# Expert stage of an attention, mixture-of-experts and MLP kernel: one matrix's loads issued one per unit, and the next expert's first token blocks transposed in units 0, 2, 3 and 5

## The chip, the cores and the metric

The kernel runs on one core of a Trainium2 chip. The metric is the device time of one execution in microseconds. The engines are named as in the profile: PE (TensorE matrix multiplies), PEld (its weight loads), DVE (VectorE), ACT (ScalarE), POOL (GpSimd) and SP (SyncE, which here only issues DMA transfers). Each engine runs its instructions in the order in which the program hands them over.

## The reference

Three stages run one after the other on 4608 rows of 512 numbers. Only the second one is touched.

```python
def _moe_ref(x, w_gate, w_noise, noise, w1, w2):   # x: (4608, 512), 8 experts, w1: (8, 512, 1024), w2: (8, 1024, 512)
    ...                                            # noisy logits; the two best experts of a row and their weights
    for e in range(E):
        for k in range(2):
            mask = top2[:, k] == e
            h = np.maximum(x[mask] @ w1[e], 0.0)
            out[mask] += top2_w[mask, k, None] * (h @ w2[e])
```

Before it stands an attention with pooled keys and values, and the gate. After it stands a dense layer, `(h - tanh(h)) @ w_out` with `h = x @ w_in`. All three come back in 32 bits; the two matrix products of an expert run as three 16-bit products each, on values split into a high and a low half.

## The kernel before, in words

**Units.** Function `moe` walks over 8 experts. An expert has room for 1216 rows, in three groups of 512, 384 and 320 rows. A group takes 8 units, so expert e has units 0 to 23; its third group (320 rows) has units 16 to 23. The names `f` (0 to 7, the unit within the group) and the keys `(e, unit)` count them. One unit is written out as: `L1` (12 matmuls into the PSUM tile `ph`, lines 355 to 357; then `ACT L359` and `DVE L360` make the two halves of `hT`), `tr` if a block is due in this unit, `L2` of two units earlier (`LAG = 2`, lines 377 to 384), and then the jobs hung on this unit with `at`. `ph` has two buffers, so `L1` of a unit waits until `DVE L360` of the unit two before has read its buffer.

**Transposing.** `tr(i, j)` prepares block j of group i while the group before it runs. ACT and DVE write the halves of 128 rows into the tile `xp` (lines 341 and 342), SP issues a transposing DMA from `xp` into `xTp` (line 343), and POOL gathers the block after next into `xg` (line 315). `xp` has one buffer: the next `ACT L341` cannot write it before the DMA has read it. A group of 512 rows has four blocks, one of 384 or 320 rows has three. Blocks are due in the units where `j * KF // n == f`: for four blocks these are f = 0, 2, 4 and 6, for three blocks 0, 2 and 5. The only groups with four blocks are the first ones of each expert; their blocks come up while the third group of the expert before runs.

**The next expert's matrices.** `Prep` loads a matrix in four chunks of 512 KB into the tile `stage` (line 118 for the first matrix, line 120 for the second), takes the largest absolute value of each chunk (`amax`, DVE line 127, and after the fourth the line 130 that makes `cm`), turns this into a scale (`fin1` with the PE transpose of `cm` on line 170, `fin2`), and splits the chunks into `pair` (ACT line 154, DVE line 159). For the first matrix the load is in unit 0, `amax` in units 3 to 6; for the second one the load is in unit 13, `amax` of chunks 0 and 1 in unit 18 and of 2 and 3 in unit 19, `fin1` in unit 20. Expert 0 has the first matrix's jobs four units later.

**Other jobs that the text names.** `Y` writes a finished group through the tile `ys` (three buffers) to `y_d` (SP line 409). For experts 1 to 4, `Conv.split` in units 1 and 2 also writes through `ys` (ACT line 290, DVE line 291) to `ws_d` (SP line 293). Line 225 loads pieces of the third stage's matrix.

Of the kernel before, what the change touches and what calls it, by code (L numbers as in the profile page):

```python
# [37 lines left out]
def kernel(ctx, tc, q, k, v, w_gate, w_noise, noise, w1, w2, w_in, w_out, out):  # L38
# [54 lines left out]
    with ExitStack() as st:  # L93
        moe(nc, tc, st, V, z)
# [81 lines left out]
def both(g):  # L176
    for _ in g:
        pass
# [8 lines left out]
def moe(nc, tc, st, V, z):  # L187
# [8 lines left out]
    KD, KF = DM // 128, FF // 128  # L196
# [7 lines left out]
    for e in range(E):  # L204
        c = 0
# [91 lines left out]
    def at(key, f, *a):  # L297
        jobs.setdefault(key, []).append((f, a))

    def run_jobs(key, between):  # L300
        for f, a in jobs.pop(key, []):
            f(*a)
            between()
# [3 lines left out]
    def gather(k):  # L307
        if k < len(blocks):
            e, c, n = blocks[k]
            if k == 6:  # L310
                x = wk.tile([128, 2, DM], F16, name="xp", bufs=1).rearrange("p a n -> p (a n)").bitcast(F32)
            else:
                x = wk.tile([128, DM], F32, name="xg", bufs=2)
            XG[k] = x
            nc.gpsimd.indirect_dma_start(  # L315
                out=x[:n], out_offset=None, in_=x_d[:, :],
                in_offset=bass.IndirectOffsetOnAxis(ap=idx[:n, e, c:c + 1], axis=0))
# [7 lines left out]
    def tr(i, j):  # L325
        if j == 0:
            XTP[i] = wk.tile([128, 2, KD, 512], F16, name="xTp")
        x = XG.pop(first[i] + j)
        n = blocks[first[i] + j][2]
        if i == 1:  # L330
            p = ps.tile([128, KD, 128], F32, name="pt", bufs=2)
            for m in range(KD):
                nc.tensor.transpose(p[:, m, :n], x[:n, 128 * m:128 * m + 128], identf[:n, :n])
            o = XTP[i][:, :, :, 128 * j:128 * j + n]
            nc.scalar.activation(o[:, 0], p[:, :, :n], AF.Copy)
            tt(o[:, 1], p[:, :, :n], o[:, 0], op=OP.subtract)  # L336
            if j < 2:
                gather(7 + j)
            return
        xp = wk.tile([128, 2, DM], F16, name="xp", bufs=1)  # L340
        nc.scalar.activation(xp[:n, 0], x[:n], AF.Copy)  # L341
        tt(xp[:n, 1], x[:n], xp[:n, 0], op=OP.subtract)  # L342
        nc.sync.dma_start_transpose(XTP[i].rearrange("p a m n -> p (a m) n")[:, :, 128 * j:128 * j + n],
                                    xp[:n].rearrange("p a n -> p (a n)"))
        gather(first[i] + j + 2)
# [3 lines left out]
    def L1(i, f):  # L349
        e, g, c0, nt = groups[i]  # L350
        w, x = W[e, 1].pair, XTP[i]
        p = ps.tile([128, 512], F32, name="ph", bufs=2)
        for m in range(KD):
            s = slice(128 * f, 128 * f + 128)
            nc.tensor.matmul(p[:, :nt], w[:, 0, m, s], x[:, 0, m, :nt], start=(m == 0), stop=False)  # L355
            nc.tensor.matmul(p[:, :nt], w[:, 0, m, s], x[:, 1, m, :nt], start=False, stop=False)  # L356
            nc.tensor.matmul(p[:, :nt], w[:, 1, m, s], x[:, 0, m, :nt], start=False, stop=(m == KD - 1))  # L357
        h = HC[i, f] = wk.tile([128, 2, 512], F16, name="hT", bufs=5)
        nc.scalar.activation(h[:, 0, :nt], p[:, :nt], AF.Relu)  # L359
        stt(h[:, 1, :nt], p[:, :nt], 0.0, h[:, 0, :nt], op0=OP.max, op1=OP.subtract)  # L360
# [3 lines left out]
    def L2(i, f):  # L364
        e, g, c0, n = groups[i]
        w, h = W[e, 2].pair.rearrange("p a b (c n) -> p a (b c) n", n=DM), HC[i, f]
        nb, half = divmod(n, 128)
        if f == 0:
            if g == 0:
                SC[e] = wk.tile([128, 1], F32, name="ysc")  # L370
                tt(SC[e], W[e, 1].sc[:, 1:2], W[e, 2].sc[:, 0:1], op=OP.mult)
            for j in range(nb + (half > 0)):
                PY[i, j] = ps.tile([128, DM], F32, name="py", bufs=4)
        for j in range(nb):
            s = slice(128 * j, 128 * j + 128)
            p = PY[i, j]
            nc.tensor.matmul(p, h[:, 0, s], w[:, 0, f], start=(f == 0), stop=False)  # L377
            nc.tensor.matmul(p, h[:, 0, s], w[:, 1, f], start=False, stop=False)  # L378
            nc.tensor.matmul(p, h[:, 1, s], w[:, 0, f], start=False, stop=(f == KF - 1))  # L379
        if half and f % 2:  # L380
            terms = [(u, a, b) for u in (f - 1, f) for a, b in ((0, 0), (0, 1), (1, 0))]
            for k, (u, a, b) in enumerate(terms):
                q = 64 * (k % 2)
                nc.tensor.matmul(PY[i, nb][q:q + 64], HC[i, u][:, a, 128 * nb:n], w[:, b, u],
                                 start=(f == 1 and k < 2), stop=(f == KF - 1 and k > 3))
        if not half:
            del HC[i, f]
        elif f % 2:
            del HC[i, f - 1], HC[i, f]
        if f == KF - 1 and i > 0:  # L390
            Y(i)
# [161 lines left out]
    for e in range(E):  # L553
        if e + 1 < E:
            c1, c2 = PR[e + 1, 1], PR[e + 1, 2]
            d = 4 if e == 0 else 0
            at((e, d), c1.load)
            at((e, 7 + d), lambda c=c1: both(c.fin1()))
            at((e, 8 + d), lambda c=c1: both(c.fin2()))
            for c in range(4):  # L560
                at((e, 3 + d + c), c1.amax, c)
                at((e, (12 if d else 10) + c), c1.split, c)
                at((e, 18 + c // 2), c2.amax, c)
                at((e, 22 + c // 2), c2.split, c)
            at((e, 15 if d else 13), c2.load)
            at((e, 20), lambda c=c2: both(c.fin1()))
            at((e, 21), lambda c=c2: both(c.fin2()))
        cv = Conv(e // 4, e % 4)
        for j in range(8):
            u = j + 3 if 0 < e < 5 else (j + 2 if j < 6 else j + 4) if e + 1 < E else (j + 4 if j < 5 else j + 6)  # L570
            if j < 2:
                at((e, j + 2 * (e + 1 == E)), cv.load, j)
            at((e, u), cv.conv, j)
            if j + 2 < 8:
                at((e, u), cv.load, j + 2)
        at((e, 14), cv.stat)
        at((e, 15), cv.fin1)
        at((e, 16), cv.fin2)
        at((e, 16), cv.norm)
        for j in range(4):  # L580
            at((e, 20 + j // 2), cv.split, j)
            if cv.which == 0:
                if j == 0:
                    at((e + 1, 0), cv.combos)
                at((e + 1, 1 + j // 2), cv.split, j, True)
# [11 lines left out]
    for u in range(len(units) + LAG):  # L597
        if u < len(units):
            i, f = units[u]
            L1(i, f)  # L600
            if u < KF:
                gate(4)
            n = -(-groups[i + 1][3] // 128) if i + 1 < len(groups) else 0
            if i > 0:
                for j in range(n):
                    if j * KF // n == f:
                        tr(i + 1, j)
            elif f == KF - 1:
                while not V["idx_loaded"]:
                    gate(10 ** 6, True)  # L610
                for k in range(4, 7):
                    gather(k)
        if u >= LAG and u not in (KF, KF + 1):
            L2(*units[u - LAG])
        if u == KF - 1:
            L2(*units[u - 1])
            L2(*units[u])
            for j in range(n):
                tr(1, j)
        if u in (KF, KF + 1):  # L620
            Y(0, range(2 * (u - KF), 2 * (u - KF) + 2))
        if u > LAG and units[u - LAG - 1][1] == KF - 1 and groups[units[u - LAG - 1][0]][0:2] == (E - 2, len(SIZES) - 1):
            overflow()
        if u in (1, 3):
            V["first"][1].split((u + 3) // 2)
        if u < KF:
            gate(6, u > 1)
        if u == KF + LAG:
            V["early"].close()
            V["pairs"].append(V["ew"].enter_context(tc.tile_pool(name="ew1", bufs=1, side="right")))  # L630
        if u < len(units):
            run_jobs((groups[i][0], KF * groups[i][1] + f), lambda: u < KF and gate(4))
            if u < KF:
                gate(6)
# [1086 lines left out]
```

## Time and profile before

| | before |
|---|---|
| median of 3 runs | 1829.58 us (1828.01 to 1830.68) |
| the profiled execution: time | 1828.06 us |
| its span, first to last instruction | 1826.2 us |
| PE busy | 1763.6 us (97% of the span) |
| DVE busy | 1301.2 us (71%) |
| ACT busy | 940.9 us (52%) |
| mean granted clock of TensorE | 0.992 |

The span is what the trace covers; the device time is 1.86 us longer. In the rows below, times are microseconds from the span's start. A number in square brackets is how long the engine had stood idle before the instruction, with what ended the wait behind the arrow. `SPq` is an issue on SP's queue: its second number is how long the issue took, not the transfer.

### The profile page before, as it was taken

What the parts mean: (1) busy time and instruction counts of PE and PEld (TensorE: products, weight loads), DVE (VectorE), ACT (ScalarE), POOL (GpSimd) and SP (SyncE); (2) the same over time, 40 slices, a digit from 0 to 9 for tenths busy, and PEclk for the clock granted to TensorE, in tenths of its full rate; (3) what the DMA queues carried; (4) which work ended last, traced back from release to release, by engine and by line L of the source; (5) the groups of instructions that cost most, each with busy time, mean ns of one, the idle gap of its engine ahead of it and who ended that gap; (6) DMA issues with size and microseconds to landing.
All of it is one profiled execution on the core that took longest, in us unless ns stands there. A gap on an engine that the chain in (4) does not pass through costs nothing. (4 is left out here: it accounts for less than half of the span.)

```text
span 1826.2 us, 28991 instructions
## 1 busy us (share of the span) xinstructions
PE 1763.6 (97%) x10791; PEld 1077.7 (59%) x10792; DVE 1301.2 (71%) x2640; ACT 940.9 (52%) x2249; POOL 263.2 (14%) x258
## 2 busy tenths in 40 slices
PE   7998889999999999999999999999999999999998
PEld 5998874445445454545445454566666666666664
DVE  5788867776676667566566456687878879787775
ACT  5886732443434343443424245565766657666554
POOL 2222001312113030110101012110111201010000
PEclk8999989999999999999999999999999999999999
DMA  9867223464464545454544434531313313041100
GB/s 224 236 166 205 61 74 108 141 161 130 141 187 122 183 129 165 139 147 124 146 106 121 103 110 120 118 89 34 93 38 74 83 42 91 24 93 46 37 24 25
DMA packets 264158, 203.45 MB, mean 111 GB/s; under 512 B 188160, under 2 KB 208640, under 8 KB 264000
## 3 DMA queue, kind: packets, MB, share of 16 engines
q1 hardware_dynamic: 251840, 162.16, 33.0%
q0 software_dynamic: 11904, 38.81, 8.2%
q8 instruction: 88, 1.44, 0.3%
q14 instruction: 70, 0.57, 0.1%
q10 hardware_dynamic: 256, 0.46, 0.1%
HBM read 121.82 MB, written 45.74 MB: 92 GB/s over the span
## 5 line engine op out<-in xcount | busy, mean ns | idle before, releaser
L359 ACT ACTIVATE hT<-ph 128x512 f16<-128x512 f32 (+2 forms) x192 | 96.8, 505 | 425.0 <-PE ph L357 418.8
L355 PE MATMUL ph<-xTp,pair 128*128 128x384 f16 (+2 forms) x736 | 245.2, 333 | 14.0 <-DMA xTp<-xp 4.8
L356 PE MATMUL ph<-xTp,pair 128*128 128x384 f16 (+2 forms) x736 | 244.9, 333 | 0.4 <-DVE xTp L336 0.4
L357 PE MATMUL ph<-xTp,pair 128*128 128x384 f16 (+2 forms) x736 | 244.9, 333 | 0.0
L360 DVE SCALAR_TENSOR_TENSOR hT<-ph,hT 128x512 f16<-128x512 f32 (+2 forms) x192 | 110.8, 577 | 163.3 <-ACT hT L359 161.5
L1042 PE MATMUL py<-wo,gT 128*128 128x512 f16 x576 | 218.3, 379 | 1.0 <-issue 1.0
L1040 PE MATMUL py<-wo,gT 128*128 128x512 f16 x576 | 218.3, 379 | 0.1
L377 PE MATMUL py<-pair,hT 128*128 128x512 f16 x576 | 218.3, 379 | 0.0
L378 PE MATMUL py<-pair,hT 128*128 128x512 f16 x576 | 218.3, 379 | 0.0
L379 PE MATMUL py<-pair,hT 128*128 128x512 f16 x576 | 218.3, 379 | 0.0
L1041 PE MATMUL py<-wo,gT 128*128 128x512 f16 x576 | 218.3, 379 | 0.0
L899 PEld LDWEIGHTS <-wi 128*128 128x128 f16 x1536 | 150.3, 98 | 58.5 <-issue 0.2
L315 POOL DMA_INDIRECT xg<-x_d,idx x75 | 85.5, 1139 | 669.8 <-DVE xp L342 462.3
L713 POOL DMA_INDIRECT y<-y_d,ridx x64 | 78.9, 1233 | 518.5 <-DVE y L724 240.7
L355 PEld LDWEIGHTS <-pair 128*128 128x128 f16 x768 | 75.0, 98 | 83.6 <-issue 24.9
L356 PEld LDWEIGHTS <-pair 128*128 128x128 f16 x768 | 75.1, 98 | 61.8 <-issue 6.0
L357 PEld LDWEIGHTS <-pair 128*128 128x128 f16 x768 | 75.1, 98 | 57.1 <-issue 0.6
L999 ACT ACTIVATE th<-th,bias 128x512 f32<-128x512 f32 x144 | 102.5, 712 | 3.3 <-DVE th L997 1.6
L1000 DVE SCALAR_TENSOR_TENSOR th<-th,t 128x512 f32<-128x512 f32 x144 | 98.6, 684 | 1.4 <-ACT th L999 1.4
L989 DVE TENSOR_TENSOR gT<-th,gT 128x512 f16<-128x512 f32 x144 | 98.7, 685 | 0.2 <-ACT gT L988 0.2
L996 DVE SCALAR_TENSOR_TENSOR t<-hb,cinf,hs 128x512 f32<-128x512 f32 x64 | 48.0, 749 | 70.9 <-ACT hs L995 68.8
L1314 ACT ACTIVATE at<-psc,mx 128x72 f32<-128x72 f32 x288 | 87.8, 334 | 18.6 <-DVE mx L1303 18.6
(305 smaller groups left out, 3496.6 us busy)
## 6 DMA issues: line engine op xcount, KB each, us to landing
stage<-in_moe_w SPq DMA_DIRECT2D x64, 512.0 KB
y_d<-ys SPq DMA_DIRECT2D x82, 256.0 KB
x_d<-xr SPq DMA_DIRECT2D x36, 256.0 KB
out<-o SPq DMA_DIRECT2D x36, 256.0 KB
qt<-in_q SPq DMA_DIRECT2D x32, 256.0 KB
raw<-in_moe_w_in SPq DMA_DIRECT2D x32, 256.0 KB
raw<-in_moe_w_out SPq DMA_DIRECT2D x32, 256.0 KB
kt<-in_k SPq DMA_DIRECT2D x7, 768.0 KB
```

The source lines that it names most:

```text
L355: nc.tensor.matmul(p[:, :nt], w[:, 0, m, s], x[:, 0, m, :nt], start=(m == 0), stop=False)
L356: nc.tensor.matmul(p[:, :nt], w[:, 0, m, s], x[:, 1, m, :nt], start=False, stop=False)
L357: nc.tensor.matmul(p[:, :nt], w[:, 1, m, s], x[:, 0, m, :nt], start=False, stop=(m == KD - 1))
L360: stt(h[:, 1, :nt], p[:, :nt], 0.0, h[:, 0, :nt], op0=OP.max, op1=OP.subtract)
L377: nc.tensor.matmul(p, h[:, 0, s], w[:, 0, f], start=(f == 0), stop=False)
L378: nc.tensor.matmul(p, h[:, 0, s], w[:, 1, f], start=False, stop=False)
L379: nc.tensor.matmul(p, h[:, 1, s], w[:, 0, f], start=False, stop=(f == KF - 1))
L899: nc.tensor.matmul(p, w[:, a, m], y[:, c, b, m], start=(start and m + x == 0), stop=(m == 1 and x == 2), skip_group_check=True)
L999: nc.scalar.activation(q, q, AF.Square, bias=bias[:, 2:3], scale=SP5)
L1040: nc.tensor.matmul(p, g[:, 0, s], wo[:, 0, f], start=(f == 0), stop=False)
L1041: nc.tensor.matmul(p, g[:, 0, s], wo[:, 1, f], start=False, stop=False)
L1042: nc.tensor.matmul(p, g[:, 1, s], wo[:, 0, f], start=False, stop=(f == KF - 1))
```

## The change

The loads of the first matrix of the next expert go out one chunk per unit, in units 0 to 3 (4 to 7 for expert 0), in place of four at once. And a group of four blocks has them transposed in units 0, 2, 3 and 5 in place of 0, 2, 4 and 6.

```diff
@@ -554,7 +554,8 @@
             d = 4 if e == 0 else 0
-            at((e, d), c1.load)
+            for c in range(4):
+                at((e, d + c), c1.load, [c])
             at((e, 7 + d), lambda c=c1: both(c.fin1()))
@@ -603,7 +604,7 @@
                 for j in range(n):
-                    if j * KF // n == f:
+                    if ((0, 2, 3, 5)[j] if n == 4 else j * KF // n) == f:
                         tr(i + 1, j)
```

On DVE, in units 18 to 21 of an expert, the second block's two instructions move up. The rows begin with the two `amax` of unit 18; `L360` is one row for each unit.

```order
 L127 TENSOR_REDUCE am<-stage 128x1 x2
 L360 SCALAR_TENSOR_TENSOR hT<-ph,hT 128x320
+L342 TENSOR_TENSOR xp<-xg,xp 128x512
 L127 TENSOR_REDUCE am<-stage 128x1 x2
 L130 TENSOR_REDUCE cm<-am 128x1
 L360 SCALAR_TENSOR_TENSOR hT<-ph,hT 128x320
-L342 TENSOR_TENSOR xp<-xg,xp 128x512
 L173 TENSOR_REDUCE cx<-pt 1x1
 L291 SCALAR_TENSOR_TENSOR wi<-qf,wsc,wi 128x512 x2
 L360 SCALAR_TENSOR_TENSOR hT<-ph,hT 128x320
+L342 TENSOR_TENSOR xp<-xg,xp 128x512
```

Block 2 (`L342`) now stands ahead of the last two `amax` and of `L130`; block 3 moves from unit 22 to the end of unit 21. On ACT, from the same unit 18 on, the order is:

```order
 L359 ACTIVATE hT<-ph 128x320
 L341 ACTIVATE xp<-xg 128x512
-L359 ACTIVATE hT<-ph 128x320 x2
-L341 ACTIVATE xp<-xg 128x512
+L359 ACTIVATE hT<-ph 128x320
+L341 ACTIVATE xp<-xg 128x512
+L359 ACTIVATE hT<-ph 128x320
 L290 ACTIVATE wi<-qf,wsc 128x512 x2
 L359 ACTIVATE hT<-ph 128x320
+L341 ACTIVATE xp<-xg 128x512
```

Between the `L341` of block 1 and that of block 2 there is now one `L359` where there were two. On SP, in units 0 to 2 of expert 1, the order before was:

```order
L118 DMA stage<-in_moe_w 128x1024 x4
L225 DMA raw<-in_moe_w_in 128x512
L409 DMA y_d<-ys 128x512 x2
L409 DMA y_d<-ys 64x512
L293 DMA ws_d<-ys 256x1x512 x2
L225 DMA raw<-in_moe_w_in 128x512
L343 DMA_TRANSPOSE xTp<-xp 128x8x128
```

At the same place it now is:

```order
L118 DMA stage<-in_moe_w 128x1024
L225 DMA raw<-in_moe_w_in 128x512
L409 DMA y_d<-ys 128x512 x2
L409 DMA y_d<-ys 64x512
L293 DMA ws_d<-ys 256x1x512 x2
L118 DMA stage<-in_moe_w 128x1024
L225 DMA raw<-in_moe_w_in 128x512
L343 DMA_TRANSPOSE xTp<-xp 128x8x128
L293 DMA ws_d<-ys 256x1x512 x2
L118 DMA stage<-in_moe_w 128x1024 x2
```

One load stands ahead of the `y_d` writes instead of four. PE and POOL run the same instructions in the same order as before.

## Rows read from the trace of the kernel before

**Rows 1.** Busy time by engine in the stretch 375 to 1000 us, clock, DMA.
```profile
375.00:1000.00 625.00, 612.51 (x3245) 307.20 (x3245) 406.80 (x802) 244.99 (x450) 93.92 (x81) 1.00 0.52 145
```
**Rows 2.** Waits of PE in that stretch: us in total, times, longest.
```profile
PE ph L355 <- DMA xTp<-xp: 4.8, 4, 1.4
PE ph L355 <- DVE pair L159: 3.8, 3, 1.3
PE ph L355 <- DVE hT L360: 3.7, 4, 1.8
```
**Rows 3.** Timeline of PE, third group of expert 1: start us, us, instruction.
```profile
468.97 0.27 PE L170 MATMUL pt<-identf,cm 128*1 128x128 f32 x1
...
481.37 0.38 PE L355 MATMUL ph<-xTp,pair 128*128 128x512 f16 x1 [1.40 <-DMA xTp<-xp]
```
**Rows 4.** Timeline of SP's queue, the same place: blocks 1 and 3.
```profile
463.40 1.24 SPq L343 DMA_TRANSPOSE xTp<-xp  x1
...
476.72 1.25 SPq L343 DMA_TRANSPOSE xTp<-xp  x1
```
**Rows 5.** Timeline of ACT, units 18 to 20 of expert 1.
```profile
462.03 0.62 ACT L341 ACTIVATE xp<-xg 128x512 f16<-128x512 f32 x1
464.07 0.44 ACT L359 ACTIVATE hT<-ph 128x320 f16<-128x320 f32 x1 [1.42 <-PE ph L357]
467.87 0.44 ACT L359 ACTIVATE hT<-ph 128x320 f16<-128x320 f32 x1 [3.36 <-PE ph L357]
```
**Rows 6.** Timeline of DVE, the same units.
```profile
462.68 0.69 DVE L342 TENSOR_TENSOR xp<-xg,xp 128x512 f16<-128x512 f32 x1
463.29 2.34 DVE L127 TENSOR_REDUCE am<-stage 128x1 f32<-128x1024 f32 x2
...
465.94 2.33 DVE L127 TENSOR_REDUCE am<-stage 128x1 f32<-128x1024 f32 x2
468.31 0.16 DVE L130 TENSOR_REDUCE cm<-am 128x1 f32<-128x4 f32 x1
```
**Rows 7.** Timelines of SP, ACT, DVE and PE, the same place in expert 0.
```profile
359.67 1.23 SPq L343 DMA_TRANSPOSE xTp<-xp  x1
...
364.09 0.63 ACT L341 ACTIVATE xp<-xg 128x512 f16<-128x512 f32 x1 [0.26 <-DMA xTp<-xp]
...
364.58 0.16 DVE L130 TENSOR_REDUCE cm<-am 128x1 f32<-128x4 f32 x1
...
364.80 0.27 PE L170 MATMUL pt<-identf,cm 128*1 128x128 f32 x1
```
**Rows 8.** Timelines of SP, ACT, DVE and PE, units 0 to 4 of expert 2.
```profile
487.43 2.04 SPq L118 DMA_DIRECT2D stage<-in_moe_w  x4
...
490.26 2.62 SPq L409 DMA_DIRECT2D y_d<-ys  x3
...
498.95 1.41 ACT L290 ACTIVATE ys<-qf,wsc 128x512 f16<-128x512 f32 x2 [5.86 <-DMA y_d<-ys]
...
501.60 0.63 DVE L360 SCALAR_TENSOR_TENSOR hT<-ph,hT 128x512 f16<-128x512 f32 x1
...
502.28 0.38 PE L355 MATMUL ph<-xTp,pair 128*128 128x512 f16 x1 [1.75 <-DVE hT L360]
```
**Rows 9.** Timelines of SP and DVE in expert 0, a write with no load ahead.
```profile
321.15 1.52 SPq L409 DMA_DIRECT2D y_d<-ys  x3
...
324.33 0.75 DVE L407 TENSOR_SCALAR ys<-py,ysc 128x512 f32<-128x512 f32 x1 [2.23 <-DMA y_d<-ys]
```
**Rows 10.** Timeline of PE: two long waits in the attention stage.
```profile
224.30 0.37 PE L1357 MATMUL px<-wgn,xT 128*128 128x160 f32 x1 [2.49 <-DVE lg L1374]
...
258.80 0.37 PE L1357 MATMUL px<-wgn,xT 128*128 128x160 f32 x1 [4.29 <-DVE lg L1374]
```
**Rows 11.** Stretches right behind them, columns as in rows 1.
```profile
225.60:235.80 10.20, 10.20 (x54) 10.18 (x53) 2.82 (x13) 3.89 (x19) 1.07 (x1) 0.50 0.08 28
259.70:263.10 3.40, 3.40 (x22) 3.30 (x21) 1.33 (x3) 1.20 (x2) 0.00 (x0) 0.50 0.09 33
```

## The prediction, made before the changed kernel ran

> **What bounds the kernel now.** I looked first at busy time by engine in the stretch of experts 1 to 6, where all that the change touches lies (expert 0 apart). PE is busy 612.51 of 625 us there, at full clock [rows 1]. So the expert stage is bound by PE, and all that a better order of the work around it can give back is the 12.49 us in which PE stands. The list of PE's waits says what these are [rows 2]: four times 4.8 us in all until `xTp` was transposed, three times 3.8 us put down to `DVE L159`, and four times 3.7 us until `DVE L360` had read a `ph` buffer. That makes 12.3 us.
>
> The first two are one thing. They are the seven starts of a new expert. At the one that ends expert 1, block 3 is issued at 476.72 [rows 4] and PE goes on at 481.37, after 1.40 us [rows 3]: 4.65 us from issue to use. Where the list names `L159`, that instruction works on the second matrix, which `L1` does not read, and the same transposing DMA ends at about that time; I count these three with the four, 8.6 us.
>
> The third is a queue. In expert 2 SP issues four loads of `stage` from 487.43 on, then the writes of `ys` to `y_d` at 490.26 [rows 8]. ACT's next split wants a `ys` buffer and stands 5.86 us for those writes, until 498.95; behind it in ACT's order are `L359` of unit 2, then `DVE L360` (501.60), and PE's `L1` of unit 4 has waited 1.75 us at 502.28.
>
> **The change, part by part.**
>
> *Loads one per unit.* It neither adds nor removes a transfer. A write to `y_d` with no load ahead was released 324.33 - 321.15 = 3.2 us after its issue [rows 9]; the one behind four loads took 498.95 - 490.26 = 8.7 us [rows 8]. Of these 5.5 us more, three loads of four should go: 4.1 us. PE needs 1.75 us of them, so this wait goes altogether, and so should the three smaller ones of the same kind: gain 3.7 us, bounds 0 (the writes are slow for another reason) and 3.7. What pays for it: chunk c comes c units later, but its `amax` is three units after its load. Four units and a wait of 1.75 lie between 481.37 and 502.28 [rows 3, 8], so a unit is about 4.8 us and three are 14 us, more than the 8.7 us that a transfer behind four loads needed. I cost it at nothing. If that cover failed, `DVE L127` would hold up `L360` behind it. In expert 0 the loads go to units 4 to 7 and `amax` to 7 to 10, the same distance.
>
> *Block 3 in unit 21.* It is issued one unit earlier, so the seven waits at the starts of experts go: gain 8.6 us, bounds 0 and 8.6.
>
> *Block 2 in unit 19.* Here I find a new wait. Block 1 is written in unit 18 and issued at 463.40 [rows 4]; block 2 now wants the one `xp` buffer right behind ACT's `L359` of unit 19, which ends at 464.07 + 0.44 = 464.5 [rows 5]. But the DMA has not read it by then. In expert 0 the trace shows just this wait, only hidden: issued at 359.67, ACT let go at 364.09, 4.42 us later [rows 7]. The same 4.42 us put ACT's `L341` of block 2 at 467.82. ACT's own `L359` of unit 20 loses little (before, it ran at 467.87). DVE loses more, since block 2's `L342` now stands ahead of the last two `amax` and of `L130` in DVE's order. The rest is copied from the distances of before [rows 5, 6]: `L342` 0.65 us after `L341`, the first `amax` 0.61 us after that, `L130` 2.37 us after the start of that `amax`, and the PE transpose `L170` 0.22 us after `L130` [rows 7]. 467.82 + 0.65 + 0.61 + 2.37 + 0.22 = 471.67. Before, `L170` ran at 468.97 with PE never idle [rows 3]. `L170` stands in PE's order ahead of `L1` of unit 21, so all matmuls behind it wait: 2.70 us. For expert 0: 359.67 + 8.27 = 367.94 against 364.80 [rows 7], 3.14 us. The five other experts repeat expert 1's distances. Sum: 6 x 2.7 + 3.1 = 19.3 us. Bounds: with the 4.65 us that PE showed in place of 4.42 it is 20.9 us; with `xp` free 1.7 us after its issue there would be no wait at all. I take 4.42, since that row is the same place, tile and engine.
>
> The Trainium skill would price this lower: its page "DMA: Bandwidth & Descriptors" gives about 2.0 us of fixed cost for a DMA (section "Anatomy of one DMA") and 261 GB/s for a transposing one (section "Latency and other measured facts"). By these, 256 KB are free about 3.0 us after the issue, an estimate, and the sum of the seven waits would be 9.4 us. The trace's 4.42 and 4.65 us disagree, and they decide.
>
> What is late next? Block 2's DMA goes out at about 469.2 and frees `xp` by 473.6; block 3 follows in unit 21 by about 475.5, lands 4.65 us later at 480.2, and the next expert's first `L1` is due at 481.37 - 1.40 + 2.70 = 482.7. So block 3's wait stays gone, and no second wait adds to the first.
>
> *The clock.* A PE that stands for 2.7 to 3.1 us may lose its clock. In the attention stage a wait of 2.49 us and one of 4.29 us [rows 10] were each followed at once by a stretch at half clock (1.2 of 2.4 GHz), of 10.2 and 3.4 us [rows 11]; behind the wait of 1.75 us [rows 8] the clock stayed full [rows 1]. The new waits are a little longer than the shorter of the two, in a stage with denser matmuls. A stretch of 3.4 us at half clock costs 1.7 us. Bounds: none (0) and all seven (11.9 us). I take three: 5.1 us.
>
> **Sum.** +19.3 - 8.6 - 3.7 + 5.1 = +12.1 us. On the profiled execution that is a span of 1826.2 + 12.1 = 1838.3 us and a time of 1840.2. The profiled execution (1828.06) lies 1.5 us under the median of the three runs, so for the median I say 1829.6 + 12.1 = 1841.7 us, 0.7% slower.
>
> **The rivals.**
>
> 1. *The stall without the clock.* The new waits come, PE keeps full clock: +7.0 us, 1836.5. For it: matmuls on both sides are dense, while the attention stage was sparse. Against it: 2.7 is above 2.49.
>
> 2. *Half the stall.* `xp` is free sooner than 4.42 us after the issue. The sum without the clock, +7.0 us over seven places, is zero where each is 1.0 us shorter, at about 3.4 us. At the 3.2 us of the plain write [rows 9] the waits are 1.22 us shorter each, 10.8 us in all: 10.8 - 12.3 = -1.5 us, 1828.1, no change that can be told. Against it: both releases of a transposing DMA that the rows show took over 4.4 us [rows 3, 4, 7]. The Trainium skill's figures above would put it still lower, at 9.4 - 12.3 = -2.9 us, 1826.7, an estimate; the trace does not agree with them.
>
> 3. *Faster.* The same mechanism below 2.9 us (4.42 - 1.53, where the seven waits are 8.6 us, 3.7 less than the gain of 12.3). At 1.7 us and less there is no stall and the whole 12.3 us come back, 1817.3. For it speaks only that these rows show a release and not the reading of `xp` itself.
>
> 4. *The loads were not the cause.* The four waits for `L360` stay: 1841.7 + 3.7 = 1845.4. And with half clock after all seven waits, 1848.4. For it: `ws_d` writes and a `line 225` load stay in the same queue.
>
> **How the numbers follow.** The forecast, stall and one to six stretches at half clock, 0.50. Rival 1: 0.27. Rival 2: 0.11. Rival 3: 0.05. Rival 4 and its top: 0.07. The predicted time is the first case's, 1841.7. A range from 1832 to 1849 holds the forecast, rival 1 with its bounds, and rival 4, and leaves out 2 and 3 and a little on top: about 0.2. Three runs of this kernel spread by 0.15%, so 0.2% (3.7 us) is about what can be told from no change. Slower by more: 0.50 + 0.27 + 0.07 = 0.84; the same 0.11; faster 0.05.
>
> **What would show it.** In the changed kernel's list of waits: `PE L170` waiting for `DVE cm L130`, seven times, 2.5 to 3.2 us each; `ACT L341` waiting for the DMA of `xTp`, about 3.3 us each; no wait of `L355` for `xTp`, for `L159` or for `L360` in this stretch; `ACT L290` waiting less than 2 us for `y_d`. Granted clock under 1.00 somewhere between 360 and 1000 us shows the clock term right. I am wrong if `L170` waits under 1.8 us each, which would mean that `xp` is free earlier; if waits for `L360` remain, the loads did not matter; and if DVE's `L127` waits for `stage`, the loads now come too late.

## The result and the profile after

| | before | after |
|---|---|---|
| median of 6 runs each, side by side | 1828.80 us (1824.83 to 1833.19) | 1843.88 us (1838.63 to 1846.39) |
| the profiled execution: time | 1828.06 us | 1846.18 us |
| its span | 1826.2 us | 1844.3 us |
| mean granted clock of TensorE | 0.992 | 0.985 |

The changed kernel is slower: ratio 1.0078, 95% interval 1.0058 to 1.0099, or 15.1 us between the medians. Names and lines up to 557 are those of before.

**The waits.** PE's and ACT's waits from 340 to 1020 us, which hold the end of expert 0 and experts 1 to 6 of the changed kernel; columns as in [rows 2].

```profile
PE pt L170 <- DVE cm L130: 19.3, 7, 4.5
PE pt L271 <- POOL qs L255: 0.9, 1, 0.9
PE ph L355 <- DMA raw<-in_moe_w_in: 0.6, 1, 0.6
```

```profile
ACT xp L341 <- DMA xTp<-xp: 28.0, 9, 4.8
ACT ys L290 <- DMA y_d<-ys: 5.2, 4, 2.1
```

All three kinds of [rows 2] are gone: no `L355` waits for `xTp`, for `L159` or for `L360`. In their place stands one large wait that was not there, `L170` for `L130`, seven times, 19.3 us. Its cause is the first ACT row. The 0.9 us of `L271` stood in the kernel before as well, ahead of the stretch of [rows 2]; the 0.6 us of `L355` are new, and come up again under the loads.

**One of the seven, followed back.** These are the timelines of SP, ACT, DVE and PE in the third group of expert 1, the place of [rows 3 to 6].

```profile
470.86 1.23 SPq L343 DMA_TRANSPOSE xTp<-xp  x1
```

```profile
475.15 0.63 ACT L341 ACTIVATE xp<-xg 128x512 f16<-128x512 f32 x1 [3.18 <-DMA xTp<-xp]
```

```profile
475.81 0.69 DVE L342 TENSOR_TENSOR xp<-xg,xp 128x512 f16<-128x512 f32 x1 [2.33 <-ACT xp L341]
476.42 2.34 DVE L127 TENSOR_REDUCE am<-stage 128x1 f32<-128x1024 f32 x2
478.79 0.16 DVE L130 TENSOR_REDUCE cm<-am 128x1 f32<-128x4 f32 x1
```

```profile
479.00 0.27 PE L170 MATMUL pt<-identf,cm 128*1 128x128 f32 x1 [2.42 <-DVE cm L130]
...
491.61 0.39 PE L355 MATMUL ph<-xTp,pair 128*128 128x512 f16 x1
```

Read from the top: block 1's DMA is issued at 470.86 and lets go of `xp` at 475.15, 4.29 us later. ACT had stood 3.18 us for it. DVE stood 2.33 us for ACT with two `amax` queued behind; they and `L130` take until 478.95, and PE, with nothing else in its order ahead of `L170`, had stood 2.42 us. The last row is the next expert's first `L1`: it starts without a wait, where [rows 3] shows 1.40 us.

**The clock behind these waits.** This is the table of stretches right behind the seven `L170` (at 372.86, 479.00, 586.15, 690.75, 795.97, 901.03 and 1004.58 us), columns as in [rows 1]; the third number from the end is the granted clock.

```profile
373.60:377.00 3.40, 3.40 (x13) 1.68 (x12) 1.87 (x4) 1.21 (x3) 0.00 (x0) 0.50 0.14 54
479.40:482.80 3.40, 3.40 (x14) 1.72 (x12) 1.58 (x4) 0.54 (x2) 0.00 (x0) 0.50 0.22 72
586.60:590.00 3.40, 3.40 (x23) 1.65 (x21) 2.64 (x5) 1.91 (x4) 0.00 (x0) 1.00 0.19 64
691.00:694.40 3.40, 3.40 (x15) 1.87 (x13) 1.65 (x4) 0.29 (x1) 0.00 (x0) 0.50 0.25 72
796.80:800.20 3.40, 3.40 (x12) 1.53 (x11) 2.01 (x4) 1.43 (x3) 0.00 (x0) 0.51 0.12 48
901.50:905.00 3.50, 3.50 (x24) 1.71 (x22) 2.62 (x5) 2.03 (x4) 0.08 (x1) 1.00 0.18 62
1005.10:1008.50 3.40, 3.40 (x14) 1.80 (x12) 1.66 (x4) 0.74 (x2) 0.00 (x0) 0.50 0.17 63
```

Behind five of seven the clock is at half, for 3.4 us each, and PE gets 12 to 15 matmuls into the time in which it does 23 or 24 at full clock. That is 5 x 1.7 = 8.5 us.

**The sum of the two profiled executions.** The span is 18.1 us longer. Ahead of unit 8 of expert 0 lie 3.8 us that the change has no part in: the stage's first `L355` runs at 267.57 us, before at 265.42, and the next row, a stretch at the start of the expert stage ahead of any moved instruction, shows half clock, 1.7 us.

```profile
267.80:271.20 3.40, 3.40 (x10) 1.16 (x9) 2.61 (x7) 0.83 (x1) 0.00 (x0) 0.50 0.47 146
```

The rest is +19.3 for `L170`, +8.5 for the clock, +0.6 for the new wait of `L355`, -8.6 for the seven starts and -3.7 for `L360`: +16.1, with the 3.8 together 19.9, 1.8 us above the 18.1. Between the `L170` of expert 0 and that of expert 6 (364.80 to 985.84 us before, 372.86 to 1004.58 now) the rows add up to 10.9 us and the trace grew by 10.7; most of the 1.8 us lies behind 1004.58 and was not followed. The medians are 15.1 us apart.

### The profile page after: what moved, and what is told of

Same layout as the page of the kernel before. It is cut to its first block, busy times and chain, and to the rows that moved or that the text cites. A ratio compares the mean times of both kernels' runs of the same rounds, so it can differ in the third digit from the quotient of the medians.

```text
span 1844.3 us, 28985 instructions
## 1 busy us (share of the span) xinstructions
PE 1774.0 (96%) x10791; PEld 1081.5 (59%) x10792; DVE 1305.3 (71%) x2640; ACT 941.5 (51%) x2249; POOL 256.4 (14%) x258
## 5 line engine op out<-in xcount | busy, mean ns | idle before, releaser
L359 ACT ACTIVATE hT<-ph 128x512 f16<-128x512 f32 (+2 forms) x192 | 96.8, 504 | 434.3 <-PE ph L357 434.2
L355 PE MATMUL ph<-xTp,pair 128*128 128x384 f16 (+2 forms) x736 | 247.6, 336 | 1.8 <-ACT xTp L335 0.7
L357 PE MATMUL ph<-xTp,pair 128*128 128x384 f16 (+2 forms) x736 | 247.8, 337 | 0.0
L356 PE MATMUL ph<-xTp,pair 128*128 128x384 f16 (+2 forms) x736 | 247.4, 336 | 0.4 <-DVE xTp L336 0.4
L360 DVE SCALAR_TENSOR_TENSOR hT<-ph,hT 128x512 f16<-128x512 f32 (+2 forms) x192 | 110.7, 577 | 175.9 <-ACT hT L359 175.7
L315 POOL DMA_INDIRECT xg<-x_d,idx x75 | 77.6, 1035 | 695.0 <-DVE xp L342 538.7
L355 PEld LDWEIGHTS <-pair 128*128 128x128 f16 x768 | 75.7, 99 | 75.4 <-issue 17.1
```

## The experiments

Each kernel is the changed one with the edit shown, save the first two, which are the kernel before with one part of the change. All times are medians beside runs of the kernel before on the same chip.

**The loads alone.**

```diff
-            at((e, d), c1.load)
+            for c in range(4):
+                at((e, d + c), c1.load, [c])
```

> Only the loads go out one per unit; the blocks stay in units 0, 2, 4 and 6. Theory (the one xp buffer makes the loss, the loads give 3.7 us back): 1828.8 - 3.7 = 1825.1 us, no wait of L355 for L360 left in experts 1 to 4, the seven waits at the starts of experts still there (8.6 us), L170 waits under 0.5 us in unit 20. Rival (the later loads make the loss, by holding up DVE): slower than 1835 us, with DVE L127 waiting for stage.

Measured: 1824.37 us in 12 runs, before 1829.72 in 17; ratio 0.9973 (0.9960 to 0.9987). PE's waits in the expert stage:

```profile
PE ph L355 <- DMA xTp<-xp: 5.8, 5, 1.5
PE ph L355 <- DVE pair L159: 2.5, 2, 1.3
PE pt L170 <- DVE cm L130: 1.4, 1, 1.4
```

The seven starts are here as in [rows 2] (8.3 us against 8.6), and the wait for `L360` is gone. So it was the loads that held up the `y_d` writes, and this half of the change is a gain of about 5 us. One wait for `L130` is new: 1.37 us in expert 0, where under 0.5 was expected. There ACT's block 1 stands 1.87 us for the DMA of block 0, with the `amax` behind it on DVE. The late loads are not needed for this: with the blocks alone, where all four loads go out at once, ACT stands the same 1.87 us there.

**The blocks alone.**

```diff
-                    if j * KF // n == f:
+                    if ((0, 2, 3, 5)[j] if n == 4 else j * KF // n) == f:
```

> Only the blocks move to units 0, 2, 3 and 5; the four loads go out at once as before. Theory: the whole loss, without the gain of the loads: 1843.9 + 3.7 = 1847.6 us, seven waits of L170 for cm of 2.3 to 3.1 us, and half-clock stretches behind some of them. Rival (the loads make the loss): about 1829 us or below.

Measured: 1847.01 us (6 runs); ratio 1.0105 (1.0086 to 1.0123). PE's waits:

```profile
PE pt L170 <- DVE cm L130: 19.5, 7, 4.5
PE ph L355 <- DVE hT L360: 4.5, 4, 1.9
```

The whole of the new wait comes with the blocks, whatever the loads do; and the wait for `L360` is back. Half clock follows four of its seven stalls (behind 367, 582, 794 and 1002 us).

**A second buffer for block 2.** Block 2 is written to a tile that is free then, in place of `xp`.

```diff
+        if j == 2 and groups[i][3] == 512:
+            xp = wk.tile([128, DM], F32, name="qs2", bufs=1).bitcast(F16).rearrange("p (a n) -> p a n", a=2)
+        else:
             xp = wk.tile([128, 2, DM], F16, name="xp", bufs=1)
```

> The whole change, with block 2 written into another tile (qs2, same size, idle in these units) in place of xp, so that it need not wait for block 1's transposing DMA. Theory: ACT's wait in unit 19 and the seven waits of L170 go, the 12.3 us come back: 1828.8 - 12.3 = 1816.5 us, clock full through the experts. Rival (block 2's ACT and DVE work is in the way in unit 19 by itself, buffer or not): L170 still waits over 1.5 us each, over 1828 us.

Measured: 1814.17 us (6 runs); ratio 0.9924 (0.9907 to 0.9941). The lines are 3 higher here. ACT in unit 19 of expert 1, and PE's waits of the expert stage:

```profile
461.60 0.44 ACT L362 ACTIVATE hT<-ph 128x320 f16<-128x320 f32 x1 [1.43 <-PE ph L360]
461.93 0.62 ACT L344 ACTIVATE qs<-xg 128x512 f16<-128x512 f32 x1
```

```profile
PE pt L170 <- DVE cm L130: 1.3, 1, 1.3
PE ph L358 <- DMA xTp<-xp: 1.2, 1, 1.2
```

Block 2's first instruction runs right behind `hT`, with no wait, and the kernel is 29.7 us faster than the changed one, about the 27.8 us of the stalls and their half clock. The order of the instructions is the same as in the changed kernel, so the order alone costs nothing; the one `xp` buffer does.

**Block 2 in unit 20, without another buffer.**

```diff
-                    if ((0, 2, 3, 5)[j] if n == 4 else j * KF // n) == f:
+                    if ((0, 2, 4, 5)[j] if n == 4 else j * KF // n) == f:
```

> The whole change, but the blocks in units 0, 2, 4 and 5. Block 3 now follows block 2 by one unit and ACT waits for xp in unit 21, some 2.7 us, but nothing that PE needs at once stands behind it on DVE. Theory: no wait of L170, none at the starts of experts: 1816.5 us, up to 1820 if block 3 lands late. Rival (any two blocks one unit apart cost PE a wait, whatever stands behind): over 1828 us.

Measured: 1815.46 us (6 runs); ratio 0.9923 (0.9906 to 0.9939). PE's waits of the expert stage, and ACT's largest for a DMA:

```profile
PE pt L170 <- DVE cm L130: 1.0, 2, 0.6
PE ph L355 <- DMA xTp<-xp: 0.5, 1, 0.5
```

```profile
ACT xp L341 <- DMA xTp<-xp: 16.5, 10, 3.2
```

ACT still waits for `xp` ten times, seven of them now in front of block 3 (in expert 1 1.58 us, until 471.38). But in unit 21 the `amax` and `L130` are past on DVE, and PE sees nothing of it. This version needs no memory and beats both kernels.

**PE kept busy ahead of `L170`.** Ten matmuls of 512 columns, whose result nothing reads, stand in PE's order ahead of `fin1` of unit 20.

```diff
+    def fill():
+        p = ps.tile([128, 512], F32, name="pt", bufs=2)
+        w = W[now_e[0], 1].pair
+        for m in range(10):
+            nc.tensor.matmul(p, w[:, 0, 0, 0:128], w[:, 0, 1, 0:512], start=True, stop=True)
...
+            at((e, 20), fill)
```

> The whole change, with ten 512-column matmuls on PE ahead of each expert's L170 in unit 20 (2.2 us, their result is used nowhere). They run while DVE is late, so PE has next to nothing left to stand for (0 to 0.5 us in six places, up to 2.3 us in expert 0), while L170 comes no sooner. Theory (the clock's share of the loss): no half-clock stretch at six of the seven places, time 1829.7 + 7.0 = 1836.7 us. Rival (the clock costs nothing, the rest of the loss is stall): about 1844 us, as without them.

Measured: 1835.82 us (6 runs), before 1828.98; ratio 1.0034 (1.0021 to 1.0046). PE at the same place of expert 1 (`L556` is the filling), and the clock behind the seven (first and last) and at the one other drop:

```profile
468.98 2.32 PE L556 MATMUL pt<-pair 128*128 128x512 f16 x10
471.58 0.27 PE L170 MATMUL pt<-identf,cm 128*1 128x128 f32 x1 [0.28 <-DVE cm L130]
```

```profile
365.40:368.80 3.40, 3.36 (x13) 1.93 (x14) 1.98 (x4) 0.00 (x0) 0.00 (x0) 0.51 0.29 79
...
525.90:529.30 3.40, 3.40 (x11) 1.36 (x9) 2.48 (x7) 1.01 (x2) 0.00 (x0) 0.50 0.29 92
...
996.50:999.90 3.40, 3.40 (x23) 1.66 (x21) 2.65 (x5) 1.91 (x4) 0.00 (x0) 1.00 0.18 64
```

The useful matmuls start no earlier than in the changed kernel: 2.32 us of filling and 0.28 of waiting stand where 2.42 of waiting stood. Yet the kernel is 8.1 us faster than the changed one. Behind expert 0's stall (still 2.13 us) the clock falls, behind the other six it stays full; the drop at 525.9 follows two waits of 0.69 and 1.27 us at the start of expert 2's second group. So the waits cost twice: by themselves, and by the clock behind them. The size is less sure. The intervals of the two ratios leave some 4 us either way, and from the stage's first `L355` on (260.33 us here) the two profiled executions differ by only 3.2 us (1573.6 and 1576.7 us); the rest lies ahead of all that the edit touches. By the rows of the stretch from 340 to 1020 us four stretches at half clock are gone (-6.8 us), one is new (+1.7), and filling and waits take 22.9 us where the waits took 19.9.

**Block 2 behind the unit's jobs.** Its instructions come in unit 19 still, but behind the `amax`, `L130` and the other jobs of that unit.

```diff
-                        tr(i + 1, j)
+                        if n == 4 and j == 2:
+                            at((groups[i][0], KF * groups[i][1] + f), tr, i + 1, j)
+                        else:
+                            tr(i + 1, j)
```

> The whole change, but block 2's instructions stand behind the jobs of unit 19 and no longer ahead of them. ACT still waits some 3.2 us for the one xp buffer, but on DVE the last two amax and L130 come first. Theory (what stands behind the wait on DVE makes the loss, not the wait): no wait of L170 over 0.6 us, 1829.7 - 12.3 = 1817.4 us. Rival (ACT's wait itself makes the loss, through L359 of unit 20): over 1830 us.

Measured: 1817.64 us (6 runs, 1812.66 to 1825.64; the profiled one is the slowest of them); ratio 0.9929 (0.9913 to 0.9945). ACT and DVE in unit 19 of expert 1:

```profile
470.09 0.63 ACT L341 ACTIVATE xp<-xg 128x512 f16<-128x512 f32 x1 [3.18 <-DMA xTp<-xp]
```

```profile
470.71 0.16 DVE L130 TENSOR_REDUCE cm<-am 128x1 f32<-128x4 f32 x1
470.81 0.69 DVE L342 TENSOR_TENSOR xp<-xg,xp 128x512 f16<-128x512 f32 x1
```

ACT waits for `xp` to the hundredth as long as in the changed kernel, 3.18 us. But `L342` stands behind `L130` now, and almost the whole loss is gone. It is not the wait for the buffer that costs, but what stands behind the waiting instruction on DVE. PE's waits of the expert stage:

```profile
PE ph L355 <- DMA xTp<-xp: 3.7, 2, 2.8
PE pt L170 <- DVE cm L130: 2.6, 2, 1.4
```

Two waits of `L170` are over the 0.6 us expected: 1.39 us in expert 0, as with the loads alone, and 1.17 us in expert 2. The latter, and the 2.84 us of `L355` behind it, belong to the loads (see below).

**Blocks in units 0, 1, 3 and 5**, so that block 1's DMA has left `xp` by unit 19.

```diff
-                    if ((0, 2, 3, 5)[j] if n == 4 else j * KF // n) == f:
+                    if ((0, 1, 3, 5)[j] if n == 4 else j * KF // n) == f:
```

> The whole change, but the blocks in units 0, 1, 3 and 5: the pair one unit apart is now blocks 0 and 1, in units 16 and 17, where DVE has no amax. Blocks 1 and 2 are two units apart, so block 2 finds xp free. Theory: no wait of L170, 1817 us, up to 1820 since ACT's wait in unit 17 now stands ahead of the output copies of the group before. Rival (the early unit 3 for block 2 is itself the cause, by the order on DVE): L170 waits over 1 us in each expert, over 1828 us.

Measured: 1826.95 us (11 runs); ratio 0.9985 (0.9973 to 0.9997), not the 1817 to 1820 expected. PE's waits, then ACT in units 17 and 19 of expert 4, and in unit 17 of expert 0:

```profile
PE pt L170 <- DVE cm L130: 7.7, 7, 2.0
PE py L377 <- ACT ys L405: 3.1, 1, 3.1
PE ph L355 <- DMA raw<-in_moe_w_in: 2.1, 1, 2.1
```

```profile
773.71 0.63 ACT L341 ACTIVATE xp<-xg 128x512 f16<-128x512 f32 x1 [1.86 <-DMA xTp<-xp]
...
780.43 0.63 ACT L341 ACTIVATE xp<-xg 128x512 f16<-128x512 f32 x1 [1.91 <-DMA xTp<-xp]
```

```profile
359.53 0.63 ACT L341 ACTIVATE xp<-xg 128x512 f16<-128x512 f32 x1 [5.58 <-DMA xTp<-xp]
360.07 0.67 ACT L405 ACTIVATE ys<-py,ysc 128x512 f32<-128x512 f32 x1
```

I had moved block 1 away from block 2, but next to block 0. Now block 1 waits for block 0 (1.86 us in expert 4), is issued that much later, and so block 2 waits as well (1.91 us), still ahead of `L130`: `L170` then waits 1.50 us there. In expert 0, ACT's `L405` stands behind block 1's wait of 5.58 us, and PE's `L2` needs its `py` buffer: 3.10 us. The loss is of the same kind, smaller, and neither expectation came as written. In experts 4 to 6 `L170` waits about 1.5 us, in 1 to 3 only 0.3 to 0.5: the two matmuls of `L271` (1.02 us on PE, in expert 1 at 457.99) stand in unit 16 of experts 0 to 3 and in no later one. With them ACT's `L359` ahead of block 1 starts 4.60 us after block 0's first instruction in expert 1, without them 3.65 us in expert 4, so block 0's DMA has 0.95 us more. The wait of 2.15 us put down to `raw` stands in expert 2, where the loads come late (see below), and half clock follows it (granted 0.51 from 526.3 to 529.7).

## Why the prediction was right, point by point

**Block 2's new wait: right in place, and in sum by two errors that cancel.** The chain ran as written, ACT `L341`, DVE `L342`, `amax`, `L130`, `L170`, and the second buffer, unit 20 and the order behind the jobs each take it away in their own way. `xp` was let go 4.29 us after the issue where I took 4.42, and the six waits are 2.28 to 2.71 us, 14.9 in all, where I said 16.2. Expert 0's is 4.47 where I said 3.14. There block 1 is itself late, which I had not followed:

```profile
351.46 1.93 SPq L120 DMA_DIRECT2D stage<-in_moe_w  x4
353.49 2.47 SPq L343 DMA_TRANSPOSE xTp<-xp  x1
```

```profile
363.25 0.63 ACT L341 ACTIVATE xp<-xg 128x512 f16<-128x512 f32 x1 [1.85 <-DMA xTp<-xp]
```

Block 0's DMA goes out right behind four loads of the second matrix, and 9.8 us pass until ACT may write `xp` again. The trace of before has this wait too: ACT's `L341` of block 1 stands 0.64 us until 358.29, 8.55 us after the issue at 349.74. I copied the distances from there, and the 1.2 us more are most of the miss. In the nine profiles this release takes 8.6 to 9.8 us; no run shows why it varies. That the sum is 19.3 us, as forecast, is luck.

The Trainium skill's figures in "DMA: Bandwidth & Descriptors" (sections "Anatomy of one DMA" and "Latency and other measured facts"), from which I estimated 3.0 us for this release, fall short here: the traces show 4.29 us with no load ahead. The fixed cost is given there for DMAs that GpSimd issues; these come from SP.

**The starts of experts: right.** Block 3 in unit 21 takes away all seven waits, 8.6 us; PE waits for `xTp` nowhere in the stretch.

**The loads: right on the gain, not on the cost.** `L290` waits for `y_d` 5.2 us in place of 21.6, 2.1 at most, and no `L355` waits for `L360`. By the medians the loads alone brought 5.3 us (interval 2.4 to 7.3), the waits that went account for 3.7. I had named DVE's `L127` waiting for `stage` as a sign that the loads come too late. It does wait, 3.2 us in three places, and behind the longest of them, in expert 2, PE waits as well (SP, DVE and PE):

```profile
508.54 8.13 SPq L593 DMA_DIRECT2D y_d<-ys  x11
...
519.91 1.17 SPq L118 DMA_DIRECT2D stage<-in_moe_w  x2
...
522.51 1.25 SPq L343 DMA_TRANSPOSE xTp<-xp  x1
...
524.45 1.22 DVE L127 TENSOR_REDUCE am<-stage 128x1 f32<-128x1024 f32 x1 [1.98 <-DMA stage<-in_moe_w]
...
532.17 0.32 PE L355 MATMUL ph<-xTp,pair 128*128 128x384 f16 x1 [0.55 <-DMA raw<-in_moe_w_in]
```

My cover of three units, costed at nothing, left out the eleven writes of `L593`, which clear the end of `y_d` in unit 1 of expert 2 only. The loads of units 2 and 3 now stand behind them on SP, and go out so late that `amax` waits 1.98 us. The next group's last block goes out behind these two loads and two of line 225, and PE uses it 9.7 us later, 0.55 us late; the list names `raw`, which `L1` does not read. Here this costs 0.6 us, with the loads alone nothing. In the five other kernels with these loads PE stands there for 1.2 to 4.0 us, and in three of them (PE kept busy, block 2 behind the unit's jobs, units 0, 1, 3 and 5) half clock follows. In the kernel before and with the blocks alone, where the loads go out at once, `amax` does not wait and neither does PE. Moving these writes, or the loads of that one expert, is the next thing to try; no run here did it.

**The clock: the mechanism right, the size too small.** This is the step that was mis-sized: I took half clock behind three of the seven waits, 5.1 us, from two waits in the attention stage. It came behind five, 8.5 us, and the forecast of +12.1 became +16.1 by the rows and +15.1 by the medians. Five is the number of one execution: over the six runs the mean granted clock goes from 0.984 (1846.39 us) to 0.990 (1838.63 us), so it need not be five in each. Filling the waits shows that this part is the clock's and not the wait's. Which of the seven lose the clock, the length of the wait does not tell: 2.71 us at 586.15 did not, 2.42 at 479.00 did. What does tell, no run shows.

**The rivals.** No clock loss (rival 1) and a shorter stall (2 and 3) fall with the rows of the seven stretches and of the waits. Loads that are not the cause (4) falls with the loads alone. The 1848.4 us given there are rival 1 and all seven stretches (1836.5 + 11.9), without the waits for `L360`; with them it would have been 1852.1.

## What to carry to other kernels

A tile with one buffer between a writing engine and a DMA sets the least distance of two uses; move one of them closer than a release (here 4.3 us from the issue, 8.6 to 9.8 behind four loads) and the wait can be read from the trace before any run. What it costs is decided by what stands behind the waiting instruction on its engine: the same wait of ACT (3.18 us in expert 1) cost 26 us over seven places with `L130` behind it on DVE (1843.88 against 1817.64), and with `L130` ahead the kernel was within 4 us of the one with a second buffer. So before an edit like this, list for each moved instruction what it is now ahead of, and try the neighbouring slot: units 0, 2, 4 and 5 kept both gains without the loss, 0.8% faster than the kernel before. And when a load moves to a later unit, look at what else stands in its queue there, in every expert: one expert had eleven writes that the others have not.

## What was not expected of the hardware

Waits of PE of only 2.3 to 2.7 us, with dense matmuls on both sides, were followed by 3.4 us at half clock in four of six cases here and in three of six with the blocks alone. Short stalls of the engine that bounds a kernel then cost almost half as much again: 19.3 us of standing, and 8.5 us of clock.
